# Handing two elementwise passes of an offloaded exponential from VectorE to GpSimd, and offloading seven more packs

## Chip, cores, metric

One Trainium2 chip, one core of it. The metric is the device time of one execution in microseconds (us), lower is better. A time quoted is a median of three to seven executions; executions of one kernel here lie within about 1.3% of each other.

## The reference

A gated sum of two attention blocks over the same x (2048 rows, 512 columns, 32 heads of 16 columns).

```python
def _A_ref(x, wqkv, wo):                       # softmax attention
    ...
    scores = jnp.einsum("bhqd,bhkd->bhqk", q, k) * (Dh ** -0.5)
    p = _softmax(scores, axis=-1)
    o = jnp.einsum("bhqk,bhkd->bhqd", p, v)
    ...
g = _sigmoid((x * gate_w).sum(-1, keepdims=True))
return g * _A_ref(x, A_wqkv, A_wo) + (1 - g) * _B_ref(x, ...)   # _B_ref: linear attention
```

Only branch A matters here: it needs 32 x 2048 x 2048 exponentials.

## The kernel before

The scores are made in tiles of 128 keys by 512 queries. A *pack* is four heads of one key block, four tiles; there are 32 x 16 = 512 packs, 2048 tiles. ScalarE takes the exponential of most of them. A few packs (54) go to VectorE, where the program builds the exponential from integers:

```python
def dve_pack(self, n, kt, first_pv):
    ...
    for i in range(4):                                      # one head each
        m = PE matmul: scores into one of two PSUM banks (ps_mp)
        ws.append(s.op("dve", 0.72, tensor_scalar(EW[...512 columns], bank, EC, 127 * 65536, mult, add)))   # int32
    lo = low 16 bits of EW, as uint16 at a step of 4 bytes
    f  = s.op("dve", 1.25, tensor_scalar(Ef, lo, 2**-16, None, mult),            ws + [self.ed_prev], pr)  # fraction, f16
    m1 = s.op("dve", 0.71, tensor_scalar(Em, Ef, 1.0, None, subtract),           [f], pr)                  # f - 1
    t  = s.op("dve", 0.71, tensor_scalar(Et, Ef, 128*EB, 128*(EA-EB/2), mult, add), [f], pr)
    u  = s.op("dve", 1.25, tensor_tensor(Em, Ef, Em, mult), [m1], pr)
    g_ = s.op("dve", 1.25, tensor_tensor(Et, Et, Em, mult), [t, u], pr)
    for hf in range(2):                                     # halves of 1024 columns
        vs.append(s.op("dve", 1.23, scalar_tensor_tensor(ED, EW, 2**-9, Et, mult, add), [g_], pr, frees=[ew]))
    self.ed_prev = vs[-1]                                   # Ef, Em, Et exist once
    return s.op("pe", 0.32, four matmuls of ED with V into ps_ot, ...)
```

(Lambdas and slices are cut; `lo`, the PE line and the last line are abridged.)

The number after the engine, 0.72 and so on, is a duration in us that the program *books*. The program contains a small list scheduler: it simulates the five engines with the booked durations, picks an order for each engine, and emits that order as fixed instruction streams with semaphore waits. On the chip no engine can deviate from its stream. PE serves everybody from one stream: scores for ScalarE (into a ring of five banks, ps_ring), scores for packs (two banks, ps_mp), values (ps_ot), and all of branch B. When PE stands at an instruction whose bank or operand is not ready, ScalarE's next scores wait behind it.

The softmax here doesn't subtract the row's maximum and nothing guards it: scores larger than these inputs give would overflow.

Of the kernel before, what the change touches and what calls it, by code (L numbers as in the profile page):

```python
# [8 lines left out]
ALU = mybir.AluOpType  # L9
AX = mybir.AxisListType  # L10
# [7 lines left out]
QCH = 512  # L18
# [13 lines left out]
EA, EB = 0.34370964, 0.07826797  # L32


DVE_COUNT = (1, 2, 1, 1, 1, 2, 1, 2, 2, 1, 2, 2, 1, 2, 2, 2, 1, 2, 2, 1, 2, 2, 2, 1, 2, 2, 2, 1, 2, 3, 2, 2)


def dve_tiles(n):
    return ((6,), (5, 11), (4, 8, 12))[DVE_COUNT[min(n, NN - 1)] - 1]

# [194 lines left out]
class _Kernel:  # L235
# [287 lines left out]
    def main_chain(self):  # L523
        s = self.s
# [6 lines left out]
        pos = [0]  # L531
        for n in range(NN):
            pos.append(pos[-1] + 64 - 4 * len(dve_tiles(n)))
        self.ed_prev = None
        self.units = units
        groups = []
        u = 0
# [12 lines left out]
        for k, (ua, ub) in enumerate(groups):  # L550
            n = units[ua][0]
# [18 lines left out]
            def qk(x, half):  # L570
# [8 lines left out]
                        deps, prio=-1e5 + k, cols=512 if w == 2 else 1024)  # L579
# [6 lines left out]
            if ub - NSLOT >= 0:  # L586
# [5 lines left out]
                deps, prio=tu))  # L592
            for p in range(ua // 4, ub // 4 + 1):
                if 4 * p + 3 > ub or p in self.o_pv:
                    continue
                n, kt, _ = units[4 * p]
# [9 lines left out]
                def pv(p, i):  # L606
# [8 lines left out]
                                    prio=self.T0 + (4 * p + 8) * self.ut, order=[self.o_pv.get(p - 1)])  # L615
# [6 lines left out]
    def dve_pack(self, n, kt, first_pv):  # L622
        s = self.s
        g = n % NG
        cp = g // 2
        part = 0 if cp == 0 else 1
        if (cp, kt // 4) not in self.o_kT:
            self.emit_kT(cp, kt // 4)
        if (kt, part) not in self.o_V:
            self.emit_V(kt, part)  # L630
        j = dve_tiles(n).index(kt)
        nj = len(dve_tiles(n))
        a, z = self.tn(n), self.tn(n + 1)
        rel = a + (z - a) * (j / nj) - 14 if n else a + 6
        pr = rel + 12
        ew, ed = Buf(self.EW_p, 2), Buf(self.ED_p, 1)
        ws = []
        m = None
        for i in range(4):
            b = self.bank(1)  # L640
            m = s.op("pe", self.c_mm(512), lambda e, i=i, b=b: e.matmul(  # L641
                self.bk(b), self.kT[:, cp, kt * P:(kt + 1) * P], self.qT[:, n % 2, i, :], start=True, stop=True),
                self.o_qT[n] + [self.o_kT[(cp, kt // 4)]], pr, rel, alloc=[b, ew] if i == 0 else [b], cols=512,
                order=[m])
            ws.append(s.op("dve", 0.72, lambda e, i=i, b=b: e.tensor_scalar(  # L645
                self.EW[:, ew.idx, i * QCH:(i + 1) * QCH], self.bk(b), float(EC), float(127 * 65536),
                op0=ALU.mult, op1=ALU.add), [m], pr, frees=[b]))
            self.qk_dve[n] = m
        lo = lambda: self.EW[:, ew.idx, :].bitcast(dt.uint16).rearrange("p (n two) -> p n two", two=2)[:, :, 0]
        f = s.op("dve", 1.25, lambda e: e.tensor_scalar(self.Ef[:], lo(), float(2.0 ** -16), None, op0=ALU.mult),  # L650
                 ws + [self.ed_prev], pr)
        m1 = s.op("dve", 0.71, lambda e: e.tensor_scalar(self.Em[:], self.Ef[:], 1.0, None, op0=ALU.subtract), [f], pr)  # L652
        t = s.op("dve", 0.71, lambda e: e.tensor_scalar(  # L653
            self.Et[:], self.Ef[:], float(128 * EB), float(128 * (EA - EB / 2)), op0=ALU.mult, op1=ALU.add), [f], pr)
        u = s.op("dve", 1.25, lambda e: e.tensor_tensor(self.Em[:], self.Ef[:], self.Em[:], ALU.mult), [m1], pr)  # L655
        g_ = s.op("dve", 1.25, lambda e: e.tensor_tensor(self.Et[:], self.Et[:], self.Em[:], ALU.mult), [t, u], pr)  # L656
        vs = []
        for hf in range(2):
            c0 = slice(hf * 2 * QCH, (hf + 1) * 2 * QCH)
            vs.append(s.op("dve", 1.23, lambda e, c0=c0: e.scalar_tensor_tensor(  # L660
                out=self.ED[:, ed.idx, c0], in0=self.EW[:, ew.idx, c0], scalar=float(2.0 ** -9), in1=self.Et[:, c0],
                op0=ALU.mult, op1=ALU.add), [g_], pr, alloc=[ed] if hf == 0 else (), frees=[ew],
                order=vs[-1:]))
        self.ed_prev = vs[-1]

        def pv(i):
            h = 8 * cp + 2 * i + (g % 2)
            return lambda e: e.matmul(  # L668
                self.ps_ot[32 * i:32 * i + VSL, :], self.Vaug[:, kt, h, :],
                self.ED[:, ed.idx, i * QCH:(i + 1) * QCH].bitcast(dt.bfloat16),  # L670
                start=False, stop=False, tile_position=(0, 32 * i), skip_group_check=True)
        return s.op("pe", 0.32, cols=512, fns=[pv(i) for i in range(4)], deps=vs + [self.o_V[(kt, part)]], prio=pr + 5, order=[first_pv],
                    frees=[ed])
# [108 lines left out]
    def feature(self, t, qk, r, readers):  # L782
        s = self.s
        ph = Buf(self.phi_p, readers)
        fs = Buf(self.fs_p, 1)
        b, m = self.proj(lambda c: self.xT[:, c, t * P:(t + 1) * P], lambda c: self.Wp[:, c, D * qk:D * qk + D], D,
                         [self.o_wp[(qk, jc)] for jc in range(4)], r + 5, r, 2, [ph, fs])
        ex = []
        for sg in range(2):
            ex.append(s.op("act", 0.53, lambda e, sg=sg: e.activation(  # L790
                self.phi[:, ph.idx, :, sg, :], self.bk(b).rearrange("p (h f) -> p h f", f=DH), ACT.Exp,
                scale=1.0 if sg == 0 else -1.0), [m], 0, frees=[b]))
        flat = lambda: self.phi[:, ph.idx].rearrange("p h s f -> p (h s) f")
        rd = s.op("dve", 1.24, lambda e: e.tensor_reduce(self.fsum[:, fs.idx, :], flat(), AX.X, ALU.add), ex, r + 10)  # L794
        rc = s.op("dve", 0.56, lambda e: e.reciprocal(self.frec[:, fs.idx, :], self.fsum[:, fs.idx, :]), [rd], r + 10)
        sc = s.op("dve", 1.24, lambda e: e.tensor_tensor(  # L796
            flat(), flat(), self.frec[:, fs.idx, :, None].to_broadcast([P, 64, DH]), ALU.mult), [rc], r + 10,
            frees=[fs])
        return ph, sc
# [52 lines left out]
    def outputs(self):  # L852
        s = self.s
        out2d = self.out.flatten_outer_dims()

        def blocks(t):
            qc, tt = divmod(t, 4)
            c0 = slice(tt * P, (tt + 1) * P)
            bl = [(lambda pr=pr, bb=self.b_onTB[t]: self.onT_B[:, bb.idx, pr, :], pr, self.WoB, self.o_onTB[t],
                   self.b_onTB[t]) for pr in range(4)]  # L860
            for pr in range(4):
                ba = self.b_onTA[qc * 4 + pr]
                bl.append((lambda ba=ba: self.onT_A[:, ba.idx, c0], pr, self.WoA, self.o_onTA[qc * 4 + pr], ba))
            return bl

        def mms(b, bl, prio, rel, also=()):
            m = None
            for k, (src, pr, W, dep, ba) in enumerate(bl):
                m = s.op("pe", self.c_mm(512), lambda e, src=src, pr=pr, W=W, k=k: e.matmul(  # L869
                    self.bk(b), src(), W[:, pr, :], start=(k == 0), stop=(k == len(bl) - 1)),  # L870
                    [dep, self.d_woa, self.d_wob], prio, rel, alloc=[b, *also] if k == 0 else (), order=[m], cols=512,
                    frees=[ba] if ba else ())
            return m

# [5 lines left out]
        for t in range(NT):  # L880
            qc = t // 4
            ot = Buf(self.outt_p, 1)
            bl = blocks(t)
            if qc < NQC - 1:
                r = self.tn(8 * (qc + 1)) + 4 + 4 * (t % 4)
                b = self.bank(1)
                m = mms(b, bl, r + 60, r, [ot])
# [4 lines left out]
            else:  # L892
                tt = t % 4
                r = self.tn(30) + 4 + 3 * tt
                b = self.bank(1)
                m = mms(b, bl[:-1], r + 10, r)
# [3 lines left out]
                b = self.bank(1)  # L900
                m = mms(b, bl[-1:], self.tn(32), 0, [ot])
# [50 lines left out]
```

## Time and profile before

| | kernel before |
|---|---|
| time, median of 3 | 923.79 us (923.68 to 930.75) |
| ScalarE (ACT) busy | 874.7 us, 94% |
| VectorE (DVE) busy | 753.6 us, 81% |
| GpSimd (POOL) busy | 6.6 us, 1% |
| granted TensorE clock | 0.965 |

(The profiled execution took 930.25 us, its span is 928.5.)

In the profile PE is TensorE (matmuls), PEld its weight loads, DVE VectorE, ACT ScalarE and POOL GpSimd; L590 is line 590 of the kernel, and a q behind an engine's name means its sequencer, which waits and issues. "issue" is time in which an engine waited for nothing that the profile shows. The *chain that ended last* is followed back from the last instruction, at each step to what released it.

The busy times of the kernel before, with their share of the span and the number of instructions, and the chain that ended last, first by engine, then by line:

```profile
PE 785.5 (85%) x5227; PEld 238.8 (26%) x5227; DVE 753.6 (81%) x1062; ACT 874.7 (94%) x801; POOL 6.6 (1%) x10
...
ACT 63%; PE 32%; DVE 2%; SPq 1%; issue 1%; DMA 0%; ACTq 0%
ACT ET L590 60%; PE ps_ring L574 15%; PE ps_mp L462 6%; PE ps_ot L611 5%; PE ps_mp L869 3%; ACT phi L790 3%; PE ps_mp L641 2%; SPq L402 1%; DVE EW L645 1%; PE ps_ot L668 1%; PE ps_mp L844 0%; PE ps_mp L809 0%; DMA xT<-in_A_x_dram 0%; DVE fsum L794 0%; DMA out_dram<-outt 0%
```

ScalarE is the bound: the chain runs through its exponentials and, between them, through the PE work that feeds them. VectorE is hardly on it.

The groups of instructions of the kernel before that matter: line, engine, operation, output and input, shapes, count; then busy us and the mean ns of one; then the idle time before them and what ended it.

```profile
L590 ACT ACTIVATE ET<-ps_ring 128x1536 bf16<-128x1536 f32 (+1 forms) x733 | 844.7, 1242 | 35.2 <-PE ps_ring L574 27.3
...
L645 DVE TENSOR_SCALAR EW<-ps_mp 128x512 int32<-128x512 f32 x216 | 143.4, 681 | 59.7 <-PE ps_mp L641 58.7
...
L660 DVE SCALAR_TENSOR_TENSOR ED<-EW,Et 128x1024 uint16<-128x1024 int32 x108 | 129.8, 1204 | 0.1
...
L650 DVE TENSOR_SCALAR Ef<-EW 128x2048 f16<-128x2048 uint16 x54 | 65.5, 1214 | 1.1
L655 DVE TENSOR_TENSOR Em<-Ef,Em 128x2048 f16<-128x2048 f16 x54 | 65.6, 1215 | 0.0
L656 DVE TENSOR_TENSOR Et<-Et,Em 128x2048 f16<-128x2048 f16 x54 | 65.3, 1209 | 0.2
...
L652 DVE TENSOR_SCALAR Em<-Ef 128x2048 f16<-128x2048 f16 x54 | 36.7, 680 | 0.7
L653 DVE TENSOR_SCALAR Et<-Ef 128x2048 f16<-128x2048 f16 x54 | 36.9, 684 | 0.0
```

L652 and L653 are the two passes that the change moves: 0.68 us each, the cheapest of the six. The 844.7 us of L590 cover 1832 tiles, 0.461 us a tile.

### The profile page before, as it was taken

How to read it: one execution, taken by the hardware profiler on the slowest of the kernel's cores; microseconds unless marked ns; L12 is line 12 of the kernel's file. 1: busy time of each engine (PE TensorE's matmuls, PEld its weight loads, DVE VectorE, ACT ScalarE, POOL GpSimd, SP SyncE). 2: the span in 40 equal slices, each digit the busy share in tenths (PEclk: the TensorE clock that was granted, in tenths of full speed). 3: DMA queues.
4: the chain of work that ended last, by engine and by line, in shares of the span. 5: the costliest groups of instructions: out<-in, count | busy, mean ns of one | idle time of the engine just before them, and what ended most of it. 6: DMA issues, size and time to landing. Idle time of an engine off the chain costs nothing.

```text
span 928.5 us, 12587 instructions
## 1 busy us (share of the span) xinstructions
PE 785.5 (85%) x5227; PEld 238.8 (26%) x5227; DVE 753.6 (81%) x1062; ACT 874.7 (94%) x801; POOL 6.6 (1%) x10
## 2 busy tenths in 40 slices
PE   7989998888888878888888889888787979878795
PEld 2223322222222212222222222222222223222221
DVE  3887787888986887888978786898879798899895
ACT  5998999999999999999999999999999998999995
POOL 2000000000000000000000000000000000000000
PEclk9999999999999999899999999999999799999997
DMA  5131000000000000000000000000000000000000
GB/s 109 52 73 47 1 6 3 1 4 4 4 2 3 4 4 4 4 7 4 9 10 10 4 6 9 9 7 7 1 4 4 4 4 24 4 4 4 4 1 23
DMA packets 25112, 11.18 MB, mean 12 GB/s; under 512 B 18016, under 2 KB 25056, under 8 KB 25056
## 3 DMA queue, kind: packets, MB, share of 16 engines
q1 hardware_dynamic: 23472, 9.99, 4.1%
q8 instruction: 41, 0.67, 0.3%
q10 hardware_dynamic: 1584, 0.39, 0.2%
q14 instruction: 15, 0.12, 0.0%
HBM read 3.16 MB, written 2.10 MB: 6 GB/s over the span
## 4 chain that ended last, share of the span: by engine, by line
ACT 63%; PE 32%; DVE 2%; SPq 1%; issue 1%; DMA 0%; ACTq 0%
ACT ET L590 60%; PE ps_ring L574 15%; PE ps_mp L462 6%; PE ps_ot L611 5%; PE ps_mp L869 3%; ACT phi L790 3%; PE ps_mp L641 2%; SPq L402 1%; DVE EW L645 1%; PE ps_ot L668 1%; PE ps_mp L844 0%; PE ps_mp L809 0%; DMA xT<-in_A_x_dram 0%; DVE fsum L794 0%; DMA out_dram<-outt 0%
## 5 line engine op out<-in xcount | busy, mean ns | idle before, releaser
L590 ACT ACTIVATE ET<-ps_ring 128x1536 bf16<-128x1536 f32 (+1 forms) x733 | 844.7, 1242 | 35.2 <-PE ps_ring L574 27.3
L574 PE MATMUL ps_ring<-qT,kT 64*128 64x512 bf16 (+1 forms) x1832 | 415.8, 399 | 123.6 <-ACT ET L590 118.9
L574 PEld LDWEIGHTS ps_ring<-qT,kT 64*128 64x128 bf16 (+1 forms) x1832 | 105.7, 94 | 426.5 <-ACT ET L590 289.3
L645 DVE TENSOR_SCALAR EW<-ps_mp 128x512 int32<-128x512 f32 x216 | 143.4, 681 | 59.7 <-PE ps_mp L641 58.7
L611 PE MATMUL ps_ot<-ET,Vaug 128*17 128x512 bf16 x1832 | 183.1, 395 | 2.4 <-DVE T_79 L679 1.2
L660 DVE SCALAR_TENSOR_TENSOR ED<-EW,Et 128x1024 uint16<-128x1024 int32 x108 | 129.8, 1204 | 0.1
L641 PE MATMUL ps_mp<-qT,kT 128*128 128x512 bf16 x216 | 81.0, 394 | 3.4 <-DVE EW L645 2.1
L611 PEld LDWEIGHTS ps_ot<-ET,Vaug 128*17 128x17 bf16 x1832 | 43.5, 87 | 109.0 <-issue 100.6
L650 DVE TENSOR_SCALAR Ef<-EW 128x2048 f16<-128x2048 uint16 x54 | 65.5, 1214 | 1.1
L655 DVE TENSOR_TENSOR Em<-Ef,Em 128x2048 f16<-128x2048 f16 x54 | 65.6, 1215 | 0.0
L656 DVE TENSOR_TENSOR Et<-Et,Em 128x2048 f16<-128x2048 f16 x54 | 65.3, 1209 | 0.2
L794 DVE TENSOR_REDUCE fsum<-phi 128x64 f32<-128x1024 bf16 x32 | 38.8, 1213 | 8.5 <-ACT phi L790 8.5
L462 PE MATMUL ps_mp<-xT,WA 128*128 128x512 bf16 x128 | 38.2, 392 | 1.5 <-DMA xT<-in_A_x_dram 1.5
L796 DVE TENSOR_TENSOR phi<-phi,frec 128x1024 bf16<-128x1024 bf16 x32 | 38.8, 1211 | 0.1
L462 PE MATMUL ps_mp<-Wp,xT 128*128 128x512 bf16 x128 | 38.4, 383 | 0.3 <-DVE EW L645 0.3
L652 DVE TENSOR_SCALAR Em<-Ef 128x2048 f16<-128x2048 f16 x54 | 36.7, 680 | 0.7
L653 DVE TENSOR_SCALAR Et<-Ef 128x2048 f16<-128x2048 f16 x54 | 36.9, 684 | 0.0
L679 DVE STREAM_TRANSPOSE T_79<-ps_ot 128x512 f32<-128x512 f32 x32 | 22.9, 715 | 17.2 <-PE ps_ot L611 17.2
L790 ACT ACTIVATE phi<-ps_mp 128x512 bf16<-128x512 f32 x64 | 34.9, 604 | 0.9 <-PE ps_mp L462 0.9
L641 PEld LDWEIGHTS ps_mp<-qT,kT 128*128 128x128 bf16 x216 | 19.7, 97 | 39.5 <-issue 18.3
L519 DVE CAST Vaug<-ps_mp 128x128 bf16<-128x128 f32 (+1 forms) x32 | 13.3, 424 | 13.3 <-PE ps_mp L462 13.2
L869 PE MATMUL ps_mp<-WoA,onT_A 128*128 128x512 bf16 x64 | 20.0, 395 | 3.9 <-DVE onT_A L692 2.3
(66 smaller groups left out, 377.7 us busy)
## 6 DMA issues: line engine op xcount, KB each, us to landing
out_dram<-outt SPq DMA_DIRECT2D x16, 128.0 KB, 1.7
qT<-qst SPq DMA_DIRECT2D x120, 16.0 KB, 1.8
WA<-in_A_wqkv_dram SPq DMA_DIRECT2D x3, 384.0 KB, 4.2
WBV<-in_B_wqkv_dram SPq DMA_DIRECT2D x1, 512.0 KB, 4.5
WoA<-in_A_wo_dram SPq DMA_DIRECT2D x1, 512.0 KB, 3.8
WoB<-in_B_wo_dram SPq DMA_DIRECT2D x1, 512.0 KB, 4.5
WA<-in_A_wqkv_dram ACTq DMA_DIRECT2D x3, 128.0 KB, 3.2
xT<-in_A_x_dram SPq DMA_TRANSPOSE x16, 2.7
```

What stands on the lines that cost most here:

```text
L462: m = s.op("pe", self.c_mm(n), lambda e, c=c: e.matmul(self.bk(b)[:, 0:n], lhs(c), rhs(c), start=(c == 0), stop=(c == 3)), deps if c == 0 ...
L574: return lambda e: e.matmul(self.ps_ring[:, x % RING, :], self.kT[r, g // 2, kt * P:(kt + 1) * P], self.qT[r, n % 2, i, :], start=True, st ...
L590: self.o_exp.append(s.op("act", w * 0.427 + 0.09, lambda e, b0=b0, s0=s0, w=w: e.activation(self.ET[:, s0:s0 + w, :], self.ps_ring[:, b0:b ...
L611: return lambda e: e.matmul(self.ps_ot[32 * i:32 * i + VSL, :], self.Vaug[:, kt, h, :], self.ET[:, (4 * p + k) % NSLOT, :], start=(kt == 0 ...
L641: m = s.op("pe", self.c_mm(512), lambda e, i=i, b=b: e.matmul(self.bk(b), self.kT[:, cp, kt * P:(kt + 1) * P], self.qT[:, n % 2, i, :], st ...
L645: ws.append(s.op("dve", 0.72, lambda e, i=i, b=b: e.tensor_scalar(self.EW[:, ew.idx, i * QCH:(i + 1) * QCH], self.bk(b), float(EC), float( ...
L650: f = s.op("dve", 1.25, lambda e: e.tensor_scalar(self.Ef[:], lo(), float(2.0 ** -16), None, op0=ALU.mult), ws + [self.ed_prev], pr)
L655: u = s.op("dve", 1.25, lambda e: e.tensor_tensor(self.Em[:], self.Ef[:], self.Em[:], ALU.mult), [m1], pr)
L656: g_ = s.op("dve", 1.25, lambda e: e.tensor_tensor(self.Et[:], self.Et[:], self.Em[:], ALU.mult), [t, u], pr)
L660: vs.append(s.op("dve", 1.23, lambda e, c0=c0: e.scalar_tensor_tensor(out=self.ED[:, ed.idx, c0], in0=self.EW[:, ew.idx, c0], scalar=float ...
L790: ex.append(s.op("act", 0.53, lambda e, sg=sg: e.activation(self.phi[:, ph.idx, :, sg, :], self.bk(b).rearrange("p (h f) -> p h f", f=DH), ...
L869: m = s.op("pe", self.c_mm(512), lambda e, src=src, pr=pr, W=W, k=k: e.matmul(self.bk(b), src(), W[:, pr, :], start=(k == 0), stop=(k == l ...
```

## The change

Intent: VectorE's two cheap passes, Em = f - 1 and Et = a f + b, go to GpSimd, which is idle, and are computed there straight from the integers, so they need not wait for Ef. VectorE gets 1.36 us a pack back and takes more packs from ScalarE. It was described as 60 packs; its tuple sums to 61.

```diff
-DVE_COUNT = (1, 2, 1, 1, 1, 2, 1, 2, 2, 1, 2, 2, 1, 2, 2, 2, 1, 2, 2, 1, 2, 2, 2, 1, 2, 2, 2, 1, 2, 3, 2, 2)
+DVE_COUNT = (1, 2, 2, 1, 2, 2, 2, 2, 2, 2, 2, 2, 2, 2, 2, 2, 1, 2, 2, 2, 2, 2, 2, 2, 2, 2, 2, 2, 2, 2, 2, 2)
...
-        m = None
+        m = self.eq_prev                        # keeps the order of the packs' score matmuls
...
-            ws.append(s.op("dve", 0.72, ...
+            ws.append(s.op("dve", 0.67, ...      # and 1.25 -> 1.22, 1.23 -> 1.205, 1.24 -> 1.22
...
-        m1 = s.op("dve", 0.71, lambda e: e.tensor_scalar(self.Em[:], self.Ef[:], 1.0, None, op0=ALU.subtract), [f], pr)
-        t = s.op("dve", 0.71, lambda e: e.tensor_scalar(
-            self.Et[:], self.Ef[:], float(128 * EB), float(128 * (EA - EB / 2)), op0=ALU.mult, op1=ALU.add), [f], pr)
+        m1, t = [], []
+        for hf in range(2):
+            c0 = slice(hf * 2 * QCH, (hf + 1) * 2 * QCH)
+            dep = ws[2 * hf:2 * hf + 2] + [self.ed_prev]
+            m1.append(s.op("pool", 1.3, lambda e, c0=c0: e.tensor_scalar(
+                self.Em[:, c0], lo()[:, c0], float(2.0 ** -16), 1.0, op0=ALU.mult, op1=ALU.subtract), dep, pr))
+            t.append(s.op("pool", 1.3, lambda e, c0=c0: e.tensor_scalar(
+                self.Et[:, c0], lo()[:, c0], float(128 * EB * 2.0 ** -16), float(128 * (EA - EB / 2)),
+                op0=ALU.mult, op1=ALU.add), dep, pr + 1))
+        u = ... [f] + m1, pr)
+        g_ = ... t + [u], pr)
...
-                    [dep, self.d_woa, self.d_wob], prio, rel, ...
+                    [x[3] for x in bl] + [self.d_woa, self.d_wob] if k == 0 else (), prio, rel, ...
```

The last hunk is in the output projection: all waits of a group of eight matmuls now stand before its first one.

More of the change, by code (lines that the diff above doesn't have):

```diff
@@ L533, in main_chain @@
             pos.append(pos[-1] + 64 - 4 * len(dve_tiles(n)))
-        self.ed_prev = None
+        self.ed_prev = self.eq_prev = None
         self.units = units
@@ L644, in dve_pack @@
                 order=[m])
-            ws.append(s.op("dve", 0.72, lambda e, i=i, b=b: e.tensor_scalar(
+            ws.append(s.op("dve", 0.67, lambda e, i=i, b=b: e.tensor_scalar(
                 self.EW[:, ew.idx, i * QCH:(i + 1) * QCH], self.bk(b), float(EC), float(127 * 65536),
                 op0=ALU.mult, op1=ALU.add), [m], pr, frees=[b]))
-            self.qk_dve[n] = m
+            self.qk_dve[n] = self.eq_prev = m
         lo = lambda: self.EW[:, ew.idx, :].bitcast(dt.uint16).rearrange("p (n two) -> p n two", two=2)[:, :, 0]
-        f = s.op("dve", 1.25, lambda e: e.tensor_scalar(self.Ef[:], lo(), float(2.0 ** -16), None, op0=ALU.mult),
+        f = s.op("dve", 1.22, lambda e: e.tensor_scalar(self.Ef[:], lo(), float(2.0 ** -16), None, op0=ALU.mult),
                  ws + [self.ed_prev], pr)
-        m1 = s.op("dve", 0.71, lambda e: e.tensor_scalar(self.Em[:], self.Ef[:], 1.0, None, op0=ALU.subtract), [f], pr)
-        t = s.op("dve", 0.71, lambda e: e.tensor_scalar(
-            self.Et[:], self.Ef[:], float(128 * EB), float(128 * (EA - EB / 2)), op0=ALU.mult, op1=ALU.add), [f], pr)
-        u = s.op("dve", 1.25, lambda e: e.tensor_tensor(self.Em[:], self.Ef[:], self.Em[:], ALU.mult), [m1], pr)
-        g_ = s.op("dve", 1.25, lambda e: e.tensor_tensor(self.Et[:], self.Et[:], self.Em[:], ALU.mult), [t, u], pr)
+        m1, t = [], []
[7 more added lines that the diff above has]
+                op0=ALU.mult, op1=ALU.add), dep, pr + 1))
+        u = s.op("dve", 1.22, lambda e: e.tensor_tensor(self.Em[:], self.Ef[:], self.Em[:], ALU.mult), [f] + m1, pr)
+        g_ = s.op("dve", 1.22, lambda e: e.tensor_tensor(self.Et[:], self.Et[:], self.Em[:], ALU.mult), t + [u], pr)
         vs = []
@@ L659, in dve_pack @@
             c0 = slice(hf * 2 * QCH, (hf + 1) * 2 * QCH)
-            vs.append(s.op("dve", 1.23, lambda e, c0=c0: e.scalar_tensor_tensor(
+            vs.append(s.op("dve", 1.205, lambda e, c0=c0: e.scalar_tensor_tensor(
                 out=self.ED[:, ed.idx, c0], in0=self.EW[:, ew.idx, c0], scalar=float(2.0 ** -9), in1=self.Et[:, c0],
@@ L793, in feature @@
         flat = lambda: self.phi[:, ph.idx].rearrange("p h s f -> p (h s) f")
-        rd = s.op("dve", 1.24, lambda e: e.tensor_reduce(self.fsum[:, fs.idx, :], flat(), AX.X, ALU.add), ex, r + 10)
+        rd = s.op("dve", 1.22, lambda e: e.tensor_reduce(self.fsum[:, fs.idx, :], flat(), AX.X, ALU.add), ex, r + 10)
         rc = s.op("dve", 0.56, lambda e: e.reciprocal(self.frec[:, fs.idx, :], self.fsum[:, fs.idx, :]), [rd], r + 10)
-        sc = s.op("dve", 1.24, lambda e: e.tensor_tensor(
+        sc = s.op("dve", 1.22, lambda e: e.tensor_tensor(
             flat(), flat(), self.frec[:, fs.idx, :, None].to_broadcast([P, 64, DH]), ALU.mult), [rc], r + 10,
@@ L870, in mms @@
                     self.bk(b), src(), W[:, pr, :], start=(k == 0), stop=(k == len(bl) - 1)),
-                    [dep, self.d_woa, self.d_wob], prio, rel, alloc=[b, *also] if k == 0 else (), order=[m], cols=512,
+                    [x[3] for x in bl] + [self.d_woa, self.d_wob] if k == 0 else (), prio, rel, alloc=[b, *also] if k == 0 else (), order=[m], cols=512,
                     frees=[ba] if ba else ())
```

## The prediction

> **What bounds the kernel now.** ScalarE. The busy table gives ACT 874.7 us of 928.5 (94%), PE 85%, DVE 81%, POOL 1%. The chain that ended last is 63% ACT, 32% PE, 2% DVE. The groups table gives 844.7 us in 733 ET exponentials, which cover 1832 tiles (32 x 64 less 4 x 54 offloaded): 0.461 us a tile. ACT's idle time before them is only 35.2 us, mostly for score matmuls (ps_ring). VectorE has slack.
>
> **What changes.**
> 1. The new count tuple sums to 61 packs, not 60 (the old one to 54). Seven packs of four tiles leave ACT: 28 x 0.461 = 12.9 us less ACT work. With the same idle time: 923.8 - 12.9 = 910.9 us.
> 2. A pack on VectorE costs 4 x 0.681 (EW) + 1.214 (Ef) + 0.680 + 0.684 (Em, Et) + 1.215 + 1.209 + 2 x 1.204 (ED) = 10.13 us. Without Em and Et it costs 8.77. So 54 x 10.13 = 547 becomes 61 x 8.77 = 535 us; DVE busy falls from 754 to about 741 us if nothing blocks it.
> 3. GpSimd gets four 1024-element tensor_scalars a pack, 244 in all. The author books 1.3 us each. A 2048-element memset on POOL takes 1.97 us, so I estimate at least 1.0 us, and 1.1 to 1.8 with a strided read: some 270 to 430 us of POOL.
> 4. The output matmuls take all their waits before their first matmul, so none stops PE half-started: 4 us of idle before L869 at most.
> 5. Score matmuls that move from the row-paired form (415.8/1832 = 0.227 us of PE a tile) to the full one (81.0/216 = 0.375) cost PE some 4 us, off the path.
>
> **The risk.** The Trainium skill, "SBUF - State Buffer", section "Who interferes with whom", says VectorE and GpSimd share a port pair as an exclusive lock, held for the whole instruction, and that VectorE instructions in a two-port mode or with two SBUF inputs contend with GpSimd. In this trace Ef runs at two elements a cycle from a strided source (2048 in 1.21 us), which looks like such a mode; u, g and both ED passes have two SBUF inputs. The GpSimd work starts after the second EW, so about 1.4 of its 5.2 us hides under EW; up to 3.8 us a pack may hold VectorE up, 61 x 3.8 = 232 us at worst, against 928 - 754 = 175 us of VectorE idle today. So VectorE comes near to being the bound; a pack's result late would stop PE (in order) at the pack's value matmuls and then ACT.
>
> **Prediction.** Most of the 12.9 us is kept: 915 us, range 902 to 948. Faster by over 2%: 0.09; within 2%: 0.74; slower: 0.17.
>
> **What would show each step.** ET exponentials near 722, 832 us busy. EW x244, Ef x61, POOL 244 tensor_scalars near 1.3 us. DVE busy near 740 if unblocked; if the lock bites, Ef, u, g, ED or the POOL instructions grow well beyond 1.2 us (or 1.3), and waits of VectorE on POOL appear before u (Em). ACT idle before ET near 35 us if all is well; else more, with DVE and POOL on the chain. L869 waits shrink.
>
> **What would make it wrong.** GpSimd instructions of 2 us, or VectorE blocked for whole ones, putting DVE on the chain: 940 to 985 us. Or less ACT idle than now, through PE stalls removed: 900.

## More of the kernel before

From the waits of the kernel before (who waited for whom: us in total, times, longest):

```profile
ACT ET L590 <- PE ps_ring L574: 27.3, 69, 1.9
...
PEld ps_mp L641 <- DVE EW L645: 11.0, 30, 1.1
...
PE ps_mp L641 <- DVE EW L645: 2.1, 6, 0.6
```

PE seldom stands still because VectorE has not emptied a pack's bank: 11.0 and 2.1 us.

## The result

| | before | changed |
|---|---|---|
| time, median | 927.27 us (4 runs, 923.68 to 935.80) | **1235.0 us** (4 runs, 1234.21 to 1236.23) |
| ratio | | 1.330, 95% interval 1.320 to 1.341 |
| ACT / DVE / POOL busy | 874.7 / 753.6 / 6.6 us | 878.5 / 776.0 / 669.1 us |
| granted TensorE clock | 0.965 | 0.815 |

A third slower; the stated range ended at 948. A ratio here and below is the mean time of one kernel's fast runs over that of the other's fast runs of the same rounds, so it is not quite the ratio of the medians beside it.

The busy times and the chain of the changed kernel:

```profile
PE 900.1 (73%) x5227; PEld 249.6 (20%) x5227; DVE 776.0 (63%) x1017; ACT 878.5 (71%) x790; POOL 669.1 (54%) x254
...
POOL 47%; DVE 27%; PE 19%; ACT 3%; issue 3%; SPq 1%; DMA 0%; POOLq 0%; DVEq 0%; ACTq 0%
POOL Em L656 35%; POOL Et L658 12%; PE ps_ring L574 8%; DVE ED L666 8%; DVE Et L662 5%; DVE EW L645 4%; PE ps_ot L611 3%; ACT ET L590 3%; PE ps_mp L462 2%; DVE Em L661 2%; PE ps_mp L875 2%; DVE phi L802 2%; DVE fsum L800 1%; PE ps_mp L641 1%; DVE T_79 L685 1%
```

No engine is busy more than 73% of the span, and POOL, busy 54% of it, holds 47% of the chain: this is a kernel bound by a latency, not by an engine's capacity. The groups of the changed kernel (L656 and L658 are now GpSimd's Em and Et, L661 is u, L662 is g, L666 is ED; L590, L645 and L650 are the same lines as before):

```profile
L590 ACT ACTIVATE ET<-ps_ring 128x1536 bf16<-128x1536 f32 x722 | 848.0, 1239 | 333.5 <-PE ps_ring L574 328.2
L656 POOL TENSOR_SCALAR Em<-EW 128x1024 f16<-128x1024 uint16 x122 | 471.3, 3864 | 526.2 <-DVE EW L645 460.8
...
L661 DVE TENSOR_TENSOR Em<-Ef,Em 128x2048 f16<-128x2048 f16 x61 | 82.5, 1353 | 246.0 <-POOL Em L656 246.0
...
L645 DVE TENSOR_SCALAR EW<-ps_mp 128x512 int32<-128x512 f32 x244 | 162.1, 680 | 55.1 <-PE ps_mp L641 54.2
L658 POOL TENSOR_SCALAR Et<-EW 128x1024 f16<-128x1024 uint16 x122 | 191.2, 1567 | 9.7
...
L666 DVE SCALAR_TENSOR_TENSOR ED<-EW,Et 128x1024 uint16<-128x1024 int32 x122 | 146.2, 1202 | 0.2
L662 DVE TENSOR_TENSOR Et<-Et,Em 128x2048 f16<-128x2048 f16 x61 | 74.3, 1218 | 34.4 <-POOL Et L658 34.4
L650 DVE TENSOR_SCALAR Ef<-EW 128x2048 f16<-128x2048 uint16 x61 | 83.3, 1366 | 1.4
```

Two GpSimd instructions of the same shape, the same source and the same output type take very different times: Em 3.86 us, Et 1.57 us in the mean. ScalarE's idle time before its exponentials rose from 35 to 333 us, nearly all of it (328 us) for score matmuls. From the waits of the changed kernel:

```profile
ACT ET L590 <- PE ps_ring L574: 328.2, 204, 10.9
DVE Em L661 <- POOL Em L656: 246.0, 61, 7.1
...
PEld ps_mp L641 <- DVE EW L645: 62.7, 49, 6.2
...
PE ps_mp L641 <- DVE EW L645: 46.6, 18, 5.9
```

So the loss travels GpSimd, VectorE, PE, ScalarE: u waits for Em 4 us a pack (246.0/61); VectorE, in order, empties no bank meanwhile; PE, in order, stands before a pack's scores (the two lines of L641 read 11 and 2 us before, 63 and 47 now); ScalarE's scores stand behind that. Those banks are only a part of it: over all matmuls, PE stood 256 us for something that VectorE had not yet done, 9 us before.

A stretch of the changed kernel in order of time (start, duration, engine, what), GpSimd first and VectorE after it:

```profile
628.21 3.63 POOL L656 TENSOR_SCALAR Em<-EW 128x1024 f16<-128x1024 uint16 x1 [8.57 <-DVE EW L645]
631.92 1.04 POOL L658 TENSOR_SCALAR Et<-EW 128x1024 f16<-128x1024 uint16 x1
633.88 4.66 POOL L656 TENSOR_SCALAR Em<-EW 128x1024 f16<-128x1024 uint16 x1 [0.91 <-DVE EW L645]
638.62 1.04 POOL L658 TENSOR_SCALAR Et<-EW 128x1024 f16<-128x1024 uint16 x1
```

```profile
628.62 1.71 DVE L802 TENSOR_TENSOR phi<-phi,frec 128x1024 bf16<-128x1024 bf16 x1
...
633.88 1.18 DVE L650 TENSOR_SCALAR Ef<-EW 128x2048 f16<-128x2048 uint16 x1
...
638.64 2.09 DVE L661 TENSOR_TENSOR Em<-Ef,Em 128x2048 f16<-128x2048 f16 x1 [2.42 <-POOL Em L656]
```

Two things are to be seen. Undisturbed, Em takes 3.63 us and Et 1.04. And the engines get in each other's way: u started 0.02 us after an Et and took 2.09 us, 0.87 more than its 1.22; where Ef came first, Em took 4.66 us, 1.03 more than 3.63. That is the contention the prediction feared, but it is the smaller of the two: Ef and u, for instance, each grew by 0.14 to 0.15 us a pack in the mean (1.37 and 1.35 us in place of 1.21 and 1.22), while u waited 4 us a pack for Em.

### The profile page after: what moved, and what is told of

Its sections match the earlier page's. It is cut to its first block, busy times and chain, and to the rows that moved or that the text cites. A ratio compares the mean times of both kernels' runs of the same rounds, so it can differ in the third digit from the quotient of the medians.

```text
span 1232.8 us, 12894 instructions
## 1 busy us (share of the span) xinstructions
PE 900.1 (73%) x5227; PEld 249.6 (20%) x5227; DVE 776.0 (63%) x1017; ACT 878.5 (71%) x790; POOL 669.1 (54%) x254
## 4 chain that ended last, share of the span: by engine, by line
POOL 47%; DVE 27%; PE 19%; ACT 3%; issue 3%; SPq 1%; DMA 0%; POOLq 0%; DVEq 0%; ACTq 0%
POOL Em L656 35%; POOL Et L658 12%; PE ps_ring L574 8%; DVE ED L666 8%; DVE Et L662 5%; DVE EW L645 4%; PE ps_ot L611 3%; ACT ET L590 3%; PE ps_mp L462 2%; DVE Em L661 2%; PE ps_mp L875 2%; DVE phi L802 2%; DVE fsum L800 1%; PE ps_mp L641 1%; DVE T_79 L685 1%
## 5 line engine op out<-in xcount | busy, mean ns | idle before, releaser
L590 ACT ACTIVATE ET<-ps_ring 128x1536 bf16<-128x1536 f32 x722 | 848.0, 1239 | 333.5 <-PE ps_ring L574 328.2
L656 POOL TENSOR_SCALAR Em<-EW 128x1024 f16<-128x1024 uint16 x122 | 471.3, 3864 | 526.2 <-DVE EW L645 460.8
L574 PE MATMUL ps_ring<-qT,kT 64*128 64x512 bf16 (+1 forms) x1804 | 461.1, 449 | 75.5 <-ACT ET L590 62.3
L661 DVE TENSOR_TENSOR Em<-Ef,Em 128x2048 f16<-128x2048 f16 x61 | 82.5, 1353 | 246.0 <-POOL Em L656 246.0
L611 PE MATMUL ps_ot<-ET,Vaug 128*17 128x512 bf16 x1804 | 203.6, 446 | 41.4 <-DVE T_79 L685 40.9
L645 DVE TENSOR_SCALAR EW<-ps_mp 128x512 int32<-128x512 f32 x244 | 162.1, 680 | 55.1 <-PE ps_mp L641 54.2
L658 POOL TENSOR_SCALAR Et<-EW 128x1024 f16<-128x1024 uint16 x122 | 191.2, 1567 | 9.7
L641 PE MATMUL ps_mp<-qT,kT 128*128 128x512 bf16 x244 | 106.4, 454 | 97.3 <-DVE EW L645 46.6
L666 DVE SCALAR_TENSOR_TENSOR ED<-EW,Et 128x1024 uint16<-128x1024 int32 x122 | 146.2, 1202 | 0.2
L662 DVE TENSOR_TENSOR Et<-Et,Em 128x2048 f16<-128x2048 f16 x61 | 74.3, 1218 | 34.4 <-POOL Et L658 34.4
L650 DVE TENSOR_SCALAR Ef<-EW 128x2048 f16<-128x2048 uint16 x61 | 83.3, 1366 | 1.4
L641 PEld LDWEIGHTS ps_mp<-qT,kT 128*128 128x128 bf16 x244 | 23.2, 101 | 152.2 <-DVE EW L645 62.7
L674 PE MATMUL ps_ot<-ED,Vaug 128*17 128x512 bf16 x244 | 32.0, 515 | 29.4 <-DVE ED L666 29.4
L800 DVE TENSOR_REDUCE fsum<-phi 128x64 f32<-128x1024 bf16 x32 | 38.7, 1209 | 4.4 <-ACT phi L796 4.4
L462 PE MATMUL ps_mp<-WA,xT 128*128 128x128 bf16 (+1 forms) x128 | 22.9, 297 | 9.9 <-DVE Vaug L519 9.2
```

The source lines that it names most:

```text
L462: m = s.op("pe", self.c_mm(n), lambda e, c=c: e.matmul(self.bk(b)[:, 0:n], lhs(c), rhs(c), start=(c == 0), stop=(c == 3)), deps if c == 0 ...
L574: return lambda e: e.matmul(self.ps_ring[:, x % RING, :], self.kT[r, g // 2, kt * P:(kt + 1) * P], self.qT[r, n % 2, i, :], start=True, st ...
L590: self.o_exp.append(s.op("act", w * 0.427 + 0.09, lambda e, b0=b0, s0=s0, w=w: e.activation(self.ET[:, s0:s0 + w, :], self.ps_ring[:, b0:b ...
L611: return lambda e: e.matmul(self.ps_ot[32 * i:32 * i + VSL, :], self.Vaug[:, kt, h, :], self.ET[:, (4 * p + k) % NSLOT, :], start=(kt == 0 ...
L641: m = s.op("pe", self.c_mm(512), lambda e, i=i, b=b: e.matmul(self.bk(b), self.kT[:, cp, kt * P:(kt + 1) * P], self.qT[:, n % 2, i, :], st ...
L645: ws.append(s.op("dve", 0.67, lambda e, i=i, b=b: e.tensor_scalar(self.EW[:, ew.idx, i * QCH:(i + 1) * QCH], self.bk(b), float(EC), float( ...
```

## The experiments

My theory after the result (S): **the subtract** of `f * 2**-16 - 1.0` is a slow path on GpSimd, and Et is fast because it adds. Rival (R1): Em is slow because of its place, first in line, on integers just written and under a contended port. Two further questions: by which path a slow instruction on an engine that is busy only half the time costs that much (L and R2, experiments 3 to 5), and where what remains after the subtract comes from (P, Q, O, G and K, experiments 6 to 14). Each letter is spelled out in the expectation where it first stands.

### 1. Add in place of subtract (same values, same order on every engine)

```diff
-    self.Em[:, c0], lo()[:, c0], float(2.0 ** -16), 1.0, op0=ALU.mult, op1=ALU.subtract), dep, pr))
+    self.Em[:, c0], lo()[:, c0], float(2.0 ** -16), -1.0, op0=ALU.mult, op1=ALU.add), dep, pr))
```

> Only the GpSimd instruction that makes Em: multiply then subtract 1.0 becomes multiply then add -1.0; same values, same schedule on every engine. Theory S (the subtract is a slow path on GpSimd: Em took 3.63 us unblocked, Et with an add 1.04 us on the same shape and source): Em falls to about 1.04 us, POOL busy from 669 to about 260 to 330 us, ScalarE's wait before the exponentials from 333 to under 60 us, time 905 to 940 us. Rival R1 (Em is slow because it comes first and reads integers VectorE has just written, or waits for the port lock): Em stays above 3 us and the time above 1200 us.

Measured: **957.38 us** (952.28 to 963.01), before 928.35 in the same rounds, ratio 1.033 (1.027 to 1.040). The result is correct. The two GpSimd lines of this run, each with minimum, median and maximum ns:

```profile
L656 POOL TENSOR_SCALAR Em<-EW x122: 1042/1048/2127, 25.6 to 918.1; 128x1024 f16<-128x1024 uint16 x122
...
L658 POOL TENSOR_SCALAR Et<-EW x122: 1047/1047/2130, 26.7 to 922.3; 128x1024 f16<-128x1024 uint16 x122
```

Em fell from a median of 3.63 to 1.05 us and is now Et's equal. One operation of one line carries 278 of the 308 us. R1 falls. The time ended above my 905 to 940 though, and above the 948 at which the prediction's range ended (GpSimd's busy time, 359 us, was above my 260 to 330 too): something else costs. This kernel, with the add, is called *the mended kernel* below.

### 2. Subtract in both

```diff
-    float(128 * EB * 2.0 ** -16), float(128 * (EA - EB / 2)), op0=ALU.mult, op1=ALU.add), dep, pr + 1))
+    float(128 * EB * 2.0 ** -16), -float(128 * (EA - EB / 2)), op0=ALU.mult, op1=ALU.subtract), dep, pr + 1))
```

> Et on GpSimd also written with a subtract (of the negated constant, same values). Theory S: Et rises from 1.04 to about 3.6 us unblocked; a pack's chain grows by about two times 2.6 us, 61 x 5.2 = 317 us: about 1550 us. Rival R1 (it is Em's place or data): Et stays near 1.04 to 1.6 us, time near 1235 us.

Measured: 1517.34 us (one run, state unknown; correct). Et rose with it:

```profile
L658 POOL TENSOR_SCALAR Et<-EW 128x1024 f16<-128x1024 uint16 x122 | 506.7, 4153 | 9.6
L656 POOL TENSOR_SCALAR Em<-EW 128x1024 f16<-128x1024 uint16 x122 | 467.7, 3835 | 496.5 <-DVE EW L645 435.6 <-DVE ED L666 56.6
```

The second subtract costs 1517 - 1235 = 282 us, the first cost 278: the cost follows the operation, wherever it stands. Both are near 61 packs x 2 x (3.63 - 1.05) = 315 us, which means that in these plans nearly every microsecond that a pack takes longer on GpSimd comes out at the end.

### 3. The subtract stays, the booked durations are made honest

```diff
-  m1.append(s.op("pool", 1.3, ...
+  m1.append(s.op("pool", 3.7, ...
-  t.append(s.op("pool", 1.3, ...
+  t.append(s.op("pool", 1.1, ...
```

> The subtract stays; only the durations the program's scheduler books are made honest (3.7 and 1.1 us instead of 1.3), so every engine gets another order. Theory L (a serial loop: a pack's GpSimd work may not start before the last ED pass of the pack before, and GpSimd plus u, g, ED is about 20 us, 61 x 20 = 1220 us): 1150 to 1240 us, the order hardly matters. Rival R2 (the loss is a wrong order: PE is told to wait for packs too early): under 1050 us.

Measured: **1011.32 us** (1009.62 to 1014.47), ratio 1.090 (1.085 to 1.094). My theory L fell: with the very same slow instructions, knowing their length gives 224 us back. R2 is closer: the changed kernel's plan put a pack's later instructions too near to its GpSimd work on VectorE's and PE's streams, and each pack then held both up. In this run u waits only 43 us for Em in place of 246, and ScalarE 63 us for its scores in place of 328 (with 40 more behind value matmuls).

### 4. The same, and Em and Et given back earlier

```diff
-  dep = ws[2 * hf:2 * hf + 2] + [self.ed_prev]         # GpSimd waits for the last ED pass of the pack before
+  m1: ws[...] + [self.u_prev]      t: ws[...] + [self.g_prev]
-  u: Em = Ef * Em     g: Et = Et * Em     ED from Et
+  u: Ef = Ef * Em     g: Ef = Et * Ef     ED from Ef
```

> The subtract stays, honest durations as in the run beside it, and Em and Et are given back early: u and g write into Ef, so GpSimd may start the next pack after u (Em) and g (Et) instead of after ED. GpSimd's own work is then the longest part of the loop: 2 x 3.63 + 2 x 1.04 = 9.3 us, with blocking up to 11, 61 x 11 = 670 us, below ScalarE's 880. Theory L: under 1000 us, 920 to 980. If instead GpSimd's throughput or the port lock is what costs, the time stays above 1100 us.

Measured: 999.77 us (995.01 to 1003.39), ratio 1.077 (1.071 to 1.082), 12 us below experiment 3. A partial miss: the serial loop exists (GpSimd waited 260 us for ED in experiment 3, and no longer does here), but it was not what cost. VectorE's work grew instead, from 784 to 814 us, since GpSimd now also runs under g and ED (1.44 and 1.31 us in place of 1.22 and 1.21). What holds this kernel at 1000 us I did not pursue.

### 5. The mended kernel with that earlier release

The edit of experiment 4 on the kernel of experiment 1.

> The mended kernel with u and g written into Ef, so that GpSimd may start a pack after u and g of the pack before and not after its last ED pass. GpSimd waited 65 us for ED in the mended kernel, which VectorE then mostly did not wait for: 945 to 960 us if that serial wait costs little (my theory), under 935 if it was the rest of the loss. The lock may bite more, since GpSimd now may run under ED's two-input passes.

Measured: 960.91 us (958.03 to 961.67), ratio 1.032 (1.025 to 1.038), at the upper edge of what I expected: as experiment 1 within the noise. The serial wait is not where the remaining 29 us are.

### 6. The last hunk alone, on the kernel before

> The kernel before with the change's last part alone: all waits of an output matmul group ahead of its first matmul. My theory: it removes at most the 4 us of idle time before those matmuls: 0.990 to 1.003 of the kernel before, 918 to 932 us. If this part is among what made the changed kernel slow, over 935 us.

Measured: 933.24 us against 929.02, ratio 1.003 (0.998 to 1.009), just above my 918 to 932 us. No difference clear of the noise shows; the interval leaves room for a loss of up to 0.9%.

### 7. The other scheduler edits alone, on the kernel before

The slightly lower VectorE durations and the kept order of the packs' matmuls; 54 packs, nothing on GpSimd.

> The kernel before (54 packs, all six passes on VectorE) with the change's other edits to the program's scheduler alone: the slightly lower VectorE durations it books (0.72 to 0.67 and so on) and the order it keeps between the score matmuls of packs. Nothing goes to GpSimd; the instructions are the same in another order. Theory O (the order of the kernel before was tuned to its old costs, and any reshuffle loses some of it): 945 us or more, which would be most of the 28 us that the mended 54-pack kernel loses. Theory G (it is GpSimd): 0.99 to 1.01, 920 to 938 us.

Measured: **926.22 us** (921.58 to 929.58), before 930.82, ratio 0.994 (0.991 to 0.998). Theory O, that any reshuffle of a tuned order costs, falls, and G stands; this is the only part of the change that is a gain, half a per cent.

### 8. 61 packs, all six passes on VectorE

The kernel before with the changed tuple.

> The kernel before, all six passes on VectorE, with the change's count tuple: 61 packs and not 54. ScalarE loses 12.9 us of work, VectorE gains 7 x 10.13 = 71 us (busy 825 us, 89%). Theory P (with the subtract mended, what still costs is an occupied VectorE: there 788 us busy and 35 us of waits on GpSimd, 823 in all): about as slow as the mended kernel, 940 to 965 us. Theory Q (the port lock and the waits on GpSimd are what costs, by stretching a pack's chain): 912 to 930 us.

Measured: 973.93 us (971.73 to 976.34), ratio 1.047 (1.041 to 1.053). VectorE was busy 817 us, 84% of the longer span. So this tuple does overload the kernel before, by a stretch at a time: in the profile ScalarE's exponentials fill 46.2 of the 60 us from 60 on (54.3 in the kernel before) and 46.4 from 180 on (55.0). It speaks for theory P and against Q, taken by itself, though it is slower than either had it (P: up to 965 us).

### 9. 54 packs with the mended offload

The kernel of experiment 1 with the old tuple.

> The mended kernel (add in place of subtract) with the old count tuple: 54 packs. VectorE's work is 206 + 54 x 8.77 = 680 us, with the lock's share and the waits on GpSimd of the mended kernel about 42 + 31 more, 753 in all, as in the kernel before. Theory P: 0.99 to 1.01 of the kernel before, 918 to 938 us. Theory Q: 940 us or more.

Measured: 957.17 us (950.86 to 957.99), ratio 1.027 (1.021 to 1.033). VectorE was busy only 730 us, 24 less than in the kernel before, and the kernel was still 28 us slower than it. So P is not enough: with equal packs and less work for VectorE, the offload itself costs. Experiments 8 and 9 together say that each of the two, seven packs or the offload, is a loss by itself in these plans.

### 10. Contention and nothing else

The kernel before with its order on PE, VectorE and ScalarE untouched, plus four GpSimd instructions a pack whose result nobody reads (an excerpt; the scratch Ez and the count of the users of the integers' buffer EW, 6 in place of 2, are left out):

```diff
+  for hf in range(2):
+      for _ in range(2):
+          self.ez_prev = s.op("pool", 1.1, tensor_scalar(Ez, lo()[:, half], 2**-16, -1.0, mult, add),
+              ws[2 * hf:2 * hf + 2] + [self.ez_prev], pr, frees=[ew])
```

> The kernel before, in exactly its order on PE, VectorE and ScalarE, plus four idle GpSimd instructions a pack that read the same integers and write a scratch nobody reads. No engine waits for GpSimd except for the integers' buffer, which it has long given back. Only contention is added. Theory K (the port lock costs): Ef, the two 16-bit passes and u grow from 1.21 and 0.68 us by 0.2 to 0.6 us, VectorE busy from 754 to 790 or more, time 940 us or more. If contention is harmless (VectorE has slack): 0.99 to 1.01, 920 to 938 us.

Measured: **970.34 us** (966.42 to 972.3), before 930.82, ratio 1.042 (1.038 to 1.045). VectorE's busy time rose from 753.6 to 832.7 us for the same instructions. In the two traces PE, VectorE and ScalarE run the same instructions in the same order, and the only wait that the trace puts down to these GpSimd instructions is one of 0.2 us on PE's weight loads. VectorE's lines for Ef, Et, Em and phi:

```profile
L651 DVE TENSOR_SCALAR Ef<-EW 128x2048 f16<-128x2048 uint16 x54 | 81.3, 1505 | 1.1
L659 DVE TENSOR_SCALAR Et<-Ef 128x2048 f16<-128x2048 f16 x54 | 68.6, 1270 | 0.0
...
L658 DVE TENSOR_SCALAR Em<-Ef 128x2048 f16<-128x2048 f16 x54 | 63.3, 1173 | 0.7
L802 DVE TENSOR_TENSOR phi<-phi,frec 128x1024 bf16<-128x1024 bf16 x32 | 42.4, 1326 | 0.1
```

Before they took 1214, 684, 680 and 1211 ns. EW and fsum, with one input each (EW's lies in PSUM), did not grow (678 and 1209 ns, 681 and 1213 before), and nor did u (1204 ns), which theory K had among those that grow. Work that hardly anything waits for, on an idle engine, slows the kernel by 4%.

### 11. The same waits without the read

The kernel of experiment 9 in exactly its order, with GpSimd's four instructions turned into memsets. Its output is wrong, which doesn't matter for the time.

> The mended 54-pack kernel in exactly its order, with GpSimd's four instructions a pack turned into memsets of Em and Et: the same waits, nearly the same length (estimate 1.0 us, half of the 1.96 us of the 2048-element memset), but no SBUF read. The result is wrong on purpose. If the lock on the read side costs: u, phi and T go back to 1.21, 1.21 and 0.41 us and the time falls from 957 towards 930 us. If it is the waits for GpSimd and the order, not the lock: 945 to 957 us.

Measured: **939.57 us** (931.31 to 940.89), ratio 1.007 (1.002 to 1.012), against 1.027 with the read. Its lines for Ef, u and phi:

```profile
L650 DVE TENSOR_SCALAR Ef<-EW 128x2048 f16<-128x2048 uint16 x54 | 98.4, 1822 | 1.1
...
L658 DVE TENSOR_TENSOR Em<-Ef,Em 128x2048 f16<-128x2048 f16 x54 | 65.2, 1208 | 8.6 <-POOL Em L656 7.1 <-DVE Ef L650 0.5
...
L799 DVE TENSOR_TENSOR phi<-phi,frec 128x1024 bf16<-128x1024 bf16 x32 | 38.7, 1209 | 0.1
```

In experiment 9 these took 1594, 1367 and 1296 ns. Without GpSimd's read the VectorE instructions with two SBUF inputs are free again, and some two thirds of the loss are gone. How much of that is the read alone is not shown: the memsets stand under the same waits, but are somewhat shorter than the passes, 1.1 and 1.3 us in the mean against 1.4 and 1.5, and VectorE's waits for them fell from 39 to 8 us. (Experiments 9 and 11 ran in different rounds on different chips, so compare their ratios.) Ef did not recover, it got worse: a pure writer still holds it up.

### 12. Measured durations in the plan, 54 packs

The kernel of experiment 9 with GpSimd booked at 1.4 and 1.5 us, Ef at 1.6, u at 1.4, phi at 1.3.

> The mended 54-pack kernel with the durations its own trace shows, blocking included, booked in the scheduler (GpSimd 1.4 and 1.5, Ef 1.6, u 1.4, phi 1.3 us). If the loss is a plan that is too short for what happens: 930 to 945 us. If the plan does not matter: 950 to 960 us.

Measured: 938.08 us (934.29 to 943.18), ratio 1.009 (1.005 to 1.014). A plan that books the blocking wins back 19 of the 28 us (in ratios to the kernel before, 1.8 of 2.7 per cent), while VectorE is as busy as before (735 us, 730 in experiment 9).

### 13. Measured durations in the plan, 61 packs

The whole change with its subtract mended and its plan made honest.

> The whole change with the subtract mended and measured durations booked (GpSimd 1.4 and 1.5, Ef 1.6, u 1.4, phi 1.3 us), 61 packs. If the 12.9 us of ScalarE work are earned once the plan is right: 938 - 13 = 925 us, 918 to 932. If the seven more packs meet a VectorE without room for them, as with all six passes on VectorE (974 us): 938 us or more. I expect the second: 938 to 955 us.

Measured: 938.39 us (937.16 to 939.11), before 927.5, ratio 1.011 (1.005 to 1.016): at the lower edge of what I expected. The seven packs, which should have earned 13 us, earn nothing over experiment 12: ScalarE's busy time falls from 876 to 865 us, and its wait for scores grows from 30 to 40 us.

### 14. Et alone on GpSimd, 54 packs

The kernel of experiment 7 with one pass handed over, booked at 1.4 us, Ef at 1.5.

> The 926 us kernel (new costs in the plan, 54 packs) with Et alone on GpSimd, two instructions a pack, booked at 1.4 us, Ef at 1.5. VectorE loses 54 x 0.68 = 37 us of work and gets half of the lock back, some 20 us. If halving the offload makes it pay: under 921 us. If any lock on the pack's chain costs more than the pass saved: 926 to 940 us. I expect the second.

Measured: 933.71 us (933.41 to 935.44), before 927.5, ratio 1.006 (1.002 to 1.010), where the kernel it starts from had 0.994. VectorE's busy time fell by 9 us against the kernel before (744.7 to 753.6), not by 37: Em, still on VectorE, takes 0.92 us beside GpSimd and Ef 1.37. So half the offload loses too: by the ratios (1.006 and 1.009 against 0.994) it costs 1.1% over the kernel it starts from, and the whole offload with measured durations (experiment 12) 1.5%.

No version beats the kernel before by more than the half per cent of experiment 7, and none with work for GpSimd beats it at all.

## Why the prediction was wrong, point by point

- **The bound** (ScalarE, with PE in the chain): right for the kernel before. It made the sum look safe, because nothing that I costed lay on ScalarE. It did not ask what a late pack does to PE's fixed stream beyond naming it.
- **Step 1**, 61 packs and 722 exponentials: exactly so (722, and 244 EW). Their busy time was put at 832 us and read 848, though one still takes 1239 ns in the mean (1242 before): the sum counts overlaps once, and a ScalarE that waits overlaps less. "Most of the 12.9 us is kept" failed as well: experiments 12 and 13, which differ by the seven packs, take the same time (938.1 and 938.4 us). So the subtract alone doesn't explain the miss; mended, the kernel at 957 us still lies above the range.
- **Step 3 is the step that failed**: "at least 1.0 us, and 1.1 to 1.8 with a strided read: some 270 to 430 us of POOL". This was worked out from a memset and taken for both passes. It holds for the add (1.04 us undisturbed, 1.57 in the mean) and not for the subtract (3.63 us undisturbed, 3.86 in the mean); POOL was busy 669 us. The profile before had no GpSimd arithmetic from which to learn it, so the honest statement would have been that no duration was known.
- **The size of the consequence** failed with it. I wrote that instructions of 2 us or blocking would give 940 to 985 us, as if VectorE's total occupation decided. What decided was a pack's latency in streams planned for 1.3 us: experiments 1 and 2 show each subtract costing about 280 us of the 315 it adds to the packs one after another, and experiment 3 shows 224 us of the loss disappear when the plan knows the length.
- **The risk, the port lock**: real, and mis-sized. I had it hold up VectorE by "up to 3.8 us a pack". Isolated, it adds 79 us of VectorE time over 54 packs in experiment 10, 1.5 us a pack, and 40 us to the kernel. With the subtract mended, taking GpSimd's read away removes some two thirds of the remaining 28 us (experiment 11, with the reservation made there), and a plan that books the blocking about as much (experiment 12). Of the signs that I listed, Ef and u grew (1.37 and 1.35 us in the changed kernel) and g and ED did not (1.22 and 1.20): GpSimd is mostly done by then, because it may not start the next pack before ED. When it may, they grow too (experiment 4).
- **Step 4**, the gathered waits: at most 4 us predicted, nothing measured (experiment 6). **Step 5**: not tested by itself.
- **Step 2**, VectorE's saving: 741 us predicted if unblocked, 776 measured in the changed kernel and 790 in the best form of it (experiment 13): the lock gives back more than the 12 us that the sum had as a gain (Ef, u, phi and T together grew by 25 us in the changed kernel).

What the Trainium skill contributed: "SBUF - State Buffer", section "Who interferes with whom", says that VectorE and GpSimd share a port pair as an exclusive lock, that an instruction in a two-port mode contends with GpSimd, and one with two SBUF inputs only with a GpSimd instruction that reads SBUF. Experiment 11 agrees on both: without reads u and phi are back at 1208 and 1209 ns, and Ef, a one-input pass from SBUF to SBUF, still suffers (1822); that Ef runs in such a mode is inferred. "GPSIMD Engine Reference", section "4.1 Engine selection", calls one-input instructions on GpSimd roughly line-rate; with the add, 1024 elements in 1.04 us agree (VectorE's ED pass over as many takes 1.20), with the subtract they don't. And "Perfetto Trace Analysis", section "Optimizing Scalar/DVE Operations", warns that offloading between these two engines might not help because of the shared port; here it did not, in any form tried.

**What stays open**: why the subtract is slow inside GpSimd (only that multiply-then-subtract is, in either pass; a subtract by itself was not tried); what holds experiment 4 at 1000 us; and whether a tuple searched for this offload could find a plan that pays.

## What to carry to other kernels

Before work moves to an engine that has done none of its kind, measure one such instruction there, with its very operations: a subtract of 1.0 and an add of -1.0 give the same numbers here and differ by a factor of 3.5 on GpSimd. In a program with fixed instruction streams, an instruction that is longer than planned can cost nearly its whole excess each time (here some 280 of 315 us), through whoever stands behind it in order, even if its engine is idle half of the time; book measured durations, blocking included. And GpSimd beside a busy VectorE was not free capacity here: test the contention alone, with idle work that nobody waits for, before building on it.

## What the Trainium skill lacked or had wrong

- "GPSIMD Engine Reference" has no time for a multiply-subtract, and nothing that sets it apart from a multiply-add, in a one-input elementwise instruction: multiply-subtract took 3.63 us on 128x1024 uint16 to f16, multiply-add 1.04 us, same data.
- "SBUF - State Buffer", section "Who interferes with whom", has the pair held for the whole instruction. For the add that nearly fits (u, started 0.02 us behind an Et of 1.04 us, took 0.87 us more, as if let go 0.90 us after the Et's start). The slow subtract held it only for part of its time: phi, started 0.41 us into an Em of 3.63 us (628.21 to 631.84), took 1.71 us in place of 1.21 and was done at 630.33, while Em was still running. The starts and ends in the four traces with undisturbed subtracts (the changed kernel, experiments 2 to 4) give a pattern. A phi that started in the first 0.74 us of one ended as if let go at 0.90 us (4 cases); of the 28 that started later, none lost more than 0.02 us. An Ef that started in the first 0.67 us was let go at 0.90 us too (32 cases); one that started between 0.95 and 1.56 us lost no more than 0.02 us (34 cases); one that started between 2.62 and 3.45 us was held until 3.50 us (25 cases). A lock for reading at the front and another for writing at the end would fit that; this reading is not tested.
- No page that was used here gives the price of the lock in a whole kernel: 216 GpSimd instructions that read SBUF, 1.40 us each in the mean with their own blocking, lengthened VectorE's work by 79 us and the kernel by 40 (experiment 10).
- Seen here and compared with no page: the granted TensorE clock was 0.965 in the kernel before (PE busy 85%), 0.815 in the changed kernel (73%) and 0.74 with two subtracts (60%). No run here separates the clock's own part in those times.
